# The opening of a Fourier-mixing and ELU kernel: seven steps' events put into one list

## The chip, the cores and the metric

The kernel runs on one core of a Trainium2 chip. The time is the device time of one execution in microseconds (us); the median of several runs is compared.

## The reference

`x` has 8 sequences of 3008 rows and 256 channels. The result is a two-layer perceptron with ELU on the real part of a two-dimensional Fourier transform:

```python
X = np.fft.fft(np.fft.fft(x, axis=1), axis=2).real
h = X.reshape(24064, 256) @ w_in             # w_in 256 x 2048
g = np.where(h > 0.0, h, np.exp(np.minimum(h, 0.0)) - 1.0)
out = g @ w_out                              # w_out 2048 x 256
```

`x` is fp32. The two weights are float64, and the kernel reads them as pairs of 32-bit words.

## The kernel before

**The transform.** `fold_x` (L498) adds and subtracts the mirrored rows and channels of one sequence: four loaded blocks L0 to L3 become the tiles e0 to e3 and o0 to o3 (and, with the short column copies c0 to c3, the sums E0, E2, O0, O2 and the four stationary tiles EO0 to EO3). For the first sequence these run on VectorE. Four `Dft` objects multiply them on TensorE with constant matrices: cosine for even rows (R_even here, R below), sine for even rows (I), cosine for odd rows (R_odd, O below), sine for odd rows (I_odd, J below). A fifth, `x_even` (x), transforms one single channel. Each has two halves of matmuls into two PSUM banks ("even" and "odd"), then `copy` (ScalarE), `unfold` (VectorE, "sum" below), and `plus` and `minus` (VectorE, "up" and "down"), which write the rings Rr, Ir and Rb in SBUF. The channel transform is put into w_in: `fold_chunk` (L427, f below) multiplies a chunk of w_in with a constant matrix, `put_chunk` copies the result to Ws and Wc on ScalarE, and `turn_last_row` and `put_last_row` (wm and wex) or `spread_last_row` (two DMAs) bring one more row into `wex`.

**Weights from 64 bits.** Each weight is read in eight chunks of 512 KB, w0 to w7 for w_in and u0 to u7 for w_out. A chunk is turned into fp32 by `fields` (VectorE: exponent, then mantissa), `power` (ScalarE, three activations), `round` (GpSimd add), and `scale` (VectorE sign, GpSimd product, for w_in also two GpSimd pair sums). Chunk w0 does all on VectorE and the exponent's activation on ScalarE.

**The perceptron.** The ring's columns are taken 256 at a time, eight steps of 256 hidden units per tile, 376 steps in all. A step is: `mm_P` (Wc by Rr into a bank H), `even_part` (V below: VectorE adds the single channel, two instructions), `mm_Q` (Ws by Ir into the same bank), `h_minus` (h: the mirrored rows), `below_plus`, `below_minus`, `exp_plus`, `exp_minus` (b+, b-, x+, x-: ScalarE), `g_plus`, `g_minus` (g+, g-: VectorE). Then the product with w_out: in the first 16 steps `mm_plain` in two halves (Xa, Xb), later a form with fewer products and four GpSimd sums. The first 16 slots alternate between tiles 0 and 1.

**PSUM.** Eight banks: three with the tag H, which P, the weight folds, the odd sine transform and others take in turn, one M, and pA to pD for the output sums. The early transforms borrow pA to pD and M.

**The order.** Most operations go through `pin`, which keeps the program order of an engine. The program order is made by `at(t, fn)`: events are sorted by t, in nominal microseconds where slot n begins at 4.8 n, and called one after another. In the profile such a time lies about 26 us later, and drifts. An event may be a group:

```python
at(-24.4, lambda: fold_now("e1 c1 E0 EO0"))
at(-10.88, w1_chunks[1].fields)      # two VectorE instructions
at(-10.5, lambda: dft_now(I_even, 0, "pC"))
```

DMAs from SP are not pinned, except those of `spread_last_row`. `load_rest` first writes one element of the sine matrix on ScalarE, which depends on x, and then loads that matrix and the next chunks.

Of the kernel before, what the change touches and what calls it, by code (L numbers as in the profile page):

```python
# [25 lines left out]
NE = 377  # L26
# [80 lines left out]
def kernel(  # L107
# [109 lines left out]
    class Chunk:  # L217
# [30 lines left out]
        def fields(self):  # L248

            if not wide:  # L250
                return
            lo, hi, dst = self.parts()
            t = spool.tile([128, 512], I32, tag=self.tmp_tag, bufs=1, name="pow2")
            self.t = t.rearrange("p (a b) -> p a b", a=dst.shape[1])
            pin(
                nc.vector.tensor_scalar(
                    out=self.t, in0=hi, scalar1=0x7FF00000, scalar2=None,
                    op0=ALU.bitwise_and,
                )
            )  # L260
            pin(
                nc.vector.tensor_scalar(
                    out=dst.bitcast(I32), in0=hi, scalar1=0xFFFFF, scalar2=0x100000,
                    op0=ALU.bitwise_and, op1=ALU.bitwise_or,
                )
            )

        def power(self):

            if not wide:  # L270
                return
            act(self.t, self.t, func=AF.Relu, scale=8.0, bias=ebias)
            if self.shared:
                lo, _, dst = self.parts()
                act(lo.bitcast(FP), lo.bitcast(U32), scale=2.0**-52)
                act(dst, dst.bitcast(I32), scale=2.0**-20)

        def round(self):

            if not wide:  # L280
                return
            lo, hi, dst = self.parts()
            if self.shared:
                gtt(dst, lo.bitcast(FP), dst, ALU.add)
                return
            pin(
                nc.vector.scalar_tensor_tensor(
                    out=dst, in0=lo.bitcast(U32), scalar=2.0**-32,
                    in1=dst.bitcast(I32), op0=ALU.mult, op1=ALU.add,
                )  # L290
            )

        def pair(self):

            dst = self.dst()
            gtt(self.ab[:, 0:256], dst[:, 0], dst[:, 1], ALU.add)
            gtt(self.ab[:, 256:512], dst[:, 0], dst[:, 1], ALU.subtract)

        def scale(self):

            self.multiply()
            if self.pairs:
                self.pair()

        def multiply(self):
            if not wide:
                return
            lo, hi, dst = self.parts()
# [5 lines left out]
            )  # L314
            if self.shared:
# [6 lines left out]
                )  # L322
            )
# [124 lines left out]

    def put_chunk(c):
        cols = slice(c * 256, (c + 1) * 256)  # L450
        for n, dst in enumerate((Ws, Wc)):
            act(dst[:, cols], folds[c][:, 256 * n : 256 * n + 256])
# [45 lines left out]
    def fold_x(L, engine_of, pieces):  # L498
# [3 lines left out]
        def op(key, o, a, b, f):  # L502
# [3 lines left out]
            n = o.shape[1]  # L506
            cuts = [n * i // pieces for i in range(pieces + 1)]
            for i in range(pieces):
# [100 lines left out]
    class Dft:  # L609
# [30 lines left out]
        def minus(self):  # L640
# [8 lines left out]
            if self.ri == 0 and not self.kodd and not self.first:  # L649
                vtt(R4[:, self.b : self.b + 1], u[:, 0:1], v[:, 0:1], ALU.subtract)  # L650
# [165 lines left out]

    def h_minus(i):
        S = steps[i]
        S.G = spool.tile([128, GW], FP, tag="G", bufs=3, name="G")
# [22 lines left out]
    def below_plus(i):  # L842
        S = steps[i]
        below(S.G[:, 512:1024], S.H)
# [262 lines left out]
    for load in loads[:5]:  # L1107
# [8 lines left out]
        L_first, lambda key: nc.vector, 1  # L1116
    )

    def fold_now(keys):
        for key in keys.split():  # L1120
            ops[key, 0]()
# [13 lines left out]
    def load_rest():  # L1135
# [7 lines left out]
        for chunk in (w1_chunks[3], w2_chunks[1], w1_chunks[4], w2_chunks[2]):  # L1143
            chunk.load()

    at(-26.9, lambda: fold_now("e3 c3 o3"))
    at(-26.8, w1_chunks[0].fields)
    at(-26.7, w1_chunks[0].power)
    at(-26.6, w1_chunks[0].round)
    at(-26.5, w1_chunks[0].scale)  # L1150
    at(-26.4, lambda: fold_now("e0 c0 e2 c2 E2"))
# [3 lines left out]
    at(-25.5, load_rest)  # L1155
    at(-24.5, begin_x_even)
    at(-24.4, lambda: fold_now("e1 c1 E0 EO0"))
    at(-20.7, lambda: load_mats(1, 1))
    at(-20.6, w1_chunks[5].load)
    at(-20.5, w2_chunks[5].load)  # L1160
    at(-13.2, lambda: fold_chunk(0))
    at(-13.1, lambda: put_chunk(0))
    at(-13.1, lambda: dft_now(state["x_even"], 0, "pC"))
    at(-13.09, lambda: state["x_even"].copy())
    at(-13.08, lambda: dft_now(state["x_even"], 1, "pD"))
    at(-13.0, lambda: dft_now(R_even, 0, "pA"))
    at(-12.9, lambda: dft_now(R_even, 1, "pB"))
    at(-11.1, lambda: fold_now("o0 o2 O2 o1 O0 EO2"))
    at(-11.0, lambda: state["x_even"].unfold())
    at(-10.95, R_even.copy)  # L1170
    at(-10.94, R_even.unfold)
    at(-10.9, R_even.plus)
    at(-10.89, lambda: state["x_even"].plus())
    at(-10.885, lambda: act(Ir[96:128, 0:NE], Rb[96:128, 0:NE]))
    at(-10.88, w1_chunks[1].fields)
    at(-10.87, w1_chunks[1].power)
    at(-10.86, w1_chunks[1].round)
    at(-10.85, R_even.minus)
    at(-10.5, lambda: dft_now(I_even, 0, "pC"))
    at(0.05, lambda: dft_now(I_even, 1, "M"))  # L1180
    at(0.6, lambda: state["x_even"].minus())
    at(0.61, lambda: act(Ir[96:128, NE:RUN], Rb[96:128, NE:RUN]))
    at(-10.84, w1_chunks[1].scale)
    at(1.3, lambda: fold_now("EO1"))

    T = PERIOD
    for chunk, k in (
        (w2_chunks[0], 0),
        (w1_chunks[2], 1),
        (w2_chunks[1], 2),  # L1190
        (w1_chunks[3], 3),
        (w2_chunks[2], 4),
        (w1_chunks[4], 5),
        (w2_chunks[3], 6),
# [9 lines left out]
        first = (  # L1204
            (0.96, 0.96, 0.97, 1.9),
            (2.1, 2.9, 2.91, 4.22),
            (2.95, 2.96, 2.97, 4.2),
            (0.95, 0.96, 0.97, 4.2),
        )
        dt = first[k] if k < 4 else (-0.5, 0.05, 0.06, 2.95)  # L1210
        for d, fn in zip(dt, (chunk.fields, chunk.power, chunk.round, chunk.scale)):
            at(t + d, fn)
    for chunk, t in (
        (w2_chunks[3], 0.5),
        (w2_chunks[4], 0.95),
# [6 lines left out]
    for c in range(1, 8):  # L1222
        at((2 * c - 2) * T + 4.7 if c > 1 else 2.7, lambda c=c: fold_chunk(c))
        t = (2 * c - 1) * T + 0.03 if c > 1 else 3.0
        at(t, lambda c=c: put_chunk(c))
        if c > 1:
            at(t + 0.01, lambda c=c: spread_last_row(c))
    at(-10.6, lambda: turn_last_row(0))
    at(-10.59, lambda: put_last_row(0))
    at(3.15, lambda: turn_last_row(1))  # L1230
    at(T + 0.25, lambda: put_last_row(1))
    for i in range(8):
        at((12.9 + 0.5 * i) * T + 3.6, lambda i=i: sum_weights(i))
    at(2 * T + 4.2, lambda: fold_now("EO3"))
# [9 lines left out]
    for slot in range(total):  # L1244
        i = slot % 2 * 8 + slot // 2 if slot < 16 else slot
        t = slot * T
        begin = (
            (0.0, mm_P),
            (0.4 if slot == 0 else 0.9, even_part),
            (2.17, mm_Q),  # L1250
            (3.55, h_minus),
            (4.2, below_plus),
            (4.8, below_minus),
            (T + 0.01 if slot < 16 else T + 1.5, exp_plus),
            (T + 0.02 if slot < 16 else T + 2.21, exp_minus),
        )
        if slot == 1:
            begin = (
                (0.1 - T, mm_P),
                (0.7 - T, even_part),  # L1260
                (2.6 - T, mm_Q),
                (1.5, h_minus),
                (2.95, below_plus),
                (3.0, below_minus),
                (3.01, exp_plus),
                (3.02, exp_minus),
            )

        X3 = ((3 * T + 0.1 if i % 8 == 0 else 2 * T + 3.05, mm_X3),)
        for dt, fn in begin + (  # L1270
            (T + 2.2, g_plus),
            (T + 2.9, g_minus),
        ) + (
            (
                (2 * T + 0.87, lambda i: mm_plain(i, 0)),
                (2 * T + 3.04, lambda i: mm_plain(i, 1)),
            )
            if i < 16
            else WINOGRAD + X3
        ):  # L1280
            at(t + dt, lambda fn=fn, i=i: fn(i))
# [59 lines left out]
    def begin_folds(b):  # L1341
        state["EO"], state["ops"] = fold_x(state["L"], lambda key: nc.gpsimd, 2)

    steps_b = HALF * 8 // TW
    for t, fn in (
        (-1.8, I_even.copy),
        (0.5, I_even.unfold),
        (0.55, I_even.plus),
        (0.65, I_even.minus),
        (3.1, lambda: dft_now(R_odd, 0, "pA")),  # L1350
        (3.2, lambda: dft_now(R_odd, 1, "pB")),
        (T + 0.005, R_odd.copy),
        (T + 1.9, R_odd.unfold),
        (T + 4.2, R_odd.plus),
        (T + 4.21, R_odd.minus),
    ):
        at(t, fn)
    at_half(3, lambda: I_odd, 0, 0)
    at_half(5, lambda: I_odd, 1, HALF)
# [25 lines left out]
    for b in range(1, NB):  # L1385
# [3 lines left out]
        at(l0 * T + 0.1, lambda b=b: state.update(zip(("L", "loads"), load_x(b))))  # L1389
        for n in range(6):  # L1390
            t = l0 + gap * n if n < 4 else l0
            at(t * T + 0.2, lambda n=n: state["loads"][n]())
# [73 lines left out]
```

## Time and profile before

| what | value |
|---|---|
| median of 7 runs | 1951.14 us (1949.22 to 1953.35) |
| profiled execution, time | 1949.54 us |
| its span | 1947.8 us |
| granted TensorE clock | 0.999 |
| first useful matmul | 14.07 us |
| P of slot 0 | 25.80 us |
| Q of slot 0 | 30.65 us |
| first X (slot 0) | 39.74 us |
| DMA in 14 to 23 us | 406 GB/s |

The profile is one execution. PE is TensorE's matmuls, PEld its weight loads, DVE VectorE, ACT ScalarE, POOL GpSimd, SP the queue that issues most DMAs. A row of the timeline has the start, the busy time, engine, line, operation, output and inputs, and in brackets the idle time before it and what ended it. The line is that of a helper where one records an operation: L410 is every matmul, L416 VectorE's additions of the transforms, L419 GpSimd's, L422 ScalarE's, L504 the folds of x, L256 and L262 a chunk's exponent and mantissa, L310 its sign, L811 V, L821 h, L837 g.

### The profile page before, as it was taken

The page shows a single profiled execution, that of the slowest core. Times are in us where ns is not written, and L with a number is a line of the kernel's source. Part 1 is how long each engine was busy: PE and PEld are TensorE (multiplying, and loading weights), DVE is VectorE, ACT ScalarE, POOL GpSimd, SP SyncE. Part 2 cuts the span into 40 slices and gives each one's busy share as a digit, 9 for nine tenths or more (in the row PEclk, how much of TensorE's full clock was granted, in tenths as well). Part 3 has the DMA queues.
Part 4 walks back from the last instruction along what each step waited for, and adds up shares of the span by engine and source line. Part 5 has one row for each costly group of instructions (what it writes and reads, how often), then busy time and mean ns, then how long its engine had stood idle before and what let it go on. Part 6 is the DMA issues. An engine that isn't in the chain of part 4 may idle for free.

```text
span 1947.8 us, 26994 instructions
## 1 busy us (share of the span) xinstructions
PE 1934.9 (99%) x8912; PEld 1653.1 (85%) x8912; DVE 1298.9 (67%) x2396; ACT 864.8 (44%) x1671; POOL 1376.4 (71%) x1816
## 2 busy tenths in 40 slices
PE   8999999999999999999999999999999999999999
PEld 5788788888888888888888888888888888888887
DVE  8966666766666666666666665676666766667666
ACT  4654444444444444444344444444434444344443
POOL 3888767776678766777677876778667776456655
PEclk9999999999999999999999999999999999999999
DMA  8146110101101121010210202012020010100101
GB/s 313 63 32 49 36 47 20 47 14 30 38 20 44 16 44 28 18 48 12 53 24 13 50 10 59 12 20 58 7 53 11 20 23 14 17 11 11 23 10 24
DMA packets 263290, 70.25 MB, mean 36 GB/s; under 512 B 248606, under 2 KB 249522, under 8 KB 263152
## 3 DMA queue, kind: packets, MB, share of 16 engines
q1 hardware_dynamic: 257360, 55.69, 15.0%
q0 software_dynamic: 3616, 12.59, 2.1%
q8 instruction: 70, 1.15, 0.3%
q14 instruction: 68, 0.56, 0.1%
q10 hardware_dynamic: 2176, 0.26, 0.1%
HBM read 43.66 MB, written 24.80 MB: 35 GB/s over the span
## 4 chain that ended last, share of the span: by engine, by line
PE 94%; DVE 3%; POOL 2%; ACT 1%; DMA 1%; issue 1%; SPq 0%; DVEq 0%
PE H L410 38%; PE pB L410 16%; PE pC L410 16%; PE pD L410 16%; PE pA L410 8%; POOL WT L419 1%; POOL G L419 0%; DMA xl<-in_x_dram 0%; DVE E L811 0%; POOL w L419 0%; DVE o L504 0%; DVE G L837 0%; DVE e L504 0%; DMA xl<-in_x_dram,ix 0%; DVE v L416 0%
## 5 line engine op out<-in xcount | busy, mean ns | idle before, releaser
L419 POOL TENSOR_TENSOR G<-G 128x256 f32<-128x256 f32 x1440 | 1034.9, 728 | 510.6 <-DVE G L837 341.3
L811 DVE SCALAR_TENSOR_TENSOR E<-Rb,wex,H 128x256 f32<-128x256 f32 x752 | 327.7, 477 | 541.5 <-PE H L410 537.3
L422 ACT ACTIVATE G<-H 128x512 f32<-128x512 f32 x376 | 224.5, 597 | 958.7 <-DVE G L821 958.7
L410 PE MATMUL H<-Ir,Ws 128*128 128x256 f32 x1504 | 387.0, 380 | 5.3 <-DVE E L811 4.2
L410 PE MATMUL H<-Rr,Wc 128*128 128x256 f32 x1504 | 386.8, 380 | 0.0
L410 PE MATMUL pC<-G,WT 128*128 128x256 f32 x1440 | 369.6, 379 | 0.0
L410 PEld LDWEIGHTS H<-Rr,Wc 128*128 128x128 f32 x1504 | 284.8, 190 | 55.3 <-issue 3.0
L410 PEld LDWEIGHTS H<-Ir,Ws 128*128 128x128 f32 x1504 | 278.4, 189 | 53.7 <-DVE E L811 6.0
L410 PEld LDWEIGHTS pC<-G,WT 128*128 128x128 f32 x1440 | 273.6, 190 | 37.2
L821 DVE SCALAR_TENSOR_TENSOR G<-E,H 128x512 f32<-128x512 f32 x376 | 256.6, 683 | 41.4 <-POOL G L419 5.0
L837 DVE SCALAR_TENSOR_TENSOR G<-G,H 128x512 f32<-128x512 f32 x376 | 255.7, 680 | 42.5 <-ACT G L422 42.5
L837 DVE SCALAR_TENSOR_TENSOR G<-M,G 128x512 f32<-128x512 f32 x376 | 256.5, 682 | 0.0
L422 ACT ACTIVATE G<-G 128x512 f32<-128x512 f32 x376 | 233.2, 620 | 0.0
L410 PE MATMUL pD<-G,w 128*128 128x256 f32 x784 | 229.4, 379 | 0.6 <-POOL G L419 0.6
L410 PE MATMUL pA<-G,w 128*128 128x256 f32 x784 | 229.3, 379 | 0.0
L410 PE MATMUL pB<-G,w 128*128 128x256 f32 x784 | 229.3, 379 | 0.0
L422 ACT ACTIVATE M<-G 128x512 f32<-128x512 f32 x376 | 224.2, 596 | 0.0
L422 ACT ACTIVATE M<-M 128x512 f32<-128x512 f32 x376 | 221.0, 588 | 0.0
L410 PE MATMUL pB<-G,WT 128*128 128x256 f32 x720 | 214.8, 380 | 0.3
L410 PE MATMUL pD<-G,WT 128*128 128x256 f32 x720 | 214.2, 379 | 0.0
L410 PEld LDWEIGHTS pD<-G,w 128*128 128x128 f32 x784 | 148.9, 190 | 21.2 <-POOL G L419 1.0
L410 PEld LDWEIGHTS pA<-G,w 128*128 128x128 f32 x784 | 148.9, 190 | 20.5 <-issue 0.3
(148 smaller groups left out, 1414.5 us busy)
## 6 DMA issues: line engine op xcount, KB each, us to landing
out_dram<-ot SPq DMA_DIRECT2D x496, 32.0 KB
xl<-in_x_dram SPq DMA_DIRECT2D x16, 512.0 KB
xl<-in_x_dram SPq DMA_DIRECT2D x16, 256.0 KB
out_dram<-ot SPq DMA_DIRECT2D x256, 2.0 KB
Rb<-r SPq DMA_DIRECT2D x10, 376.0 KB
raw<-in_moe_w_in_dram SPq DMA_DIRECT2D x7, 512.0 KB
MC<-dft_mats SPq DMA_DIRECT2D x3, 943.5 KB
raw<-in_moe_w_out_dram SPq DMA_DIRECT2D x4, 512.0 KB
```

Of the source, the lines that this page charges most:

```text
L410: nc.tensor.matmul(out_, lhsT=lhsT, rhs=rhs, start=start, stop=stop, skip_group_check=True)
L419: pin(nc.gpsimd.tensor_tensor(out=o, in0=a, in1=b, op=op))
L422: pin(nc.scalar.activation(out=o, in_=i, func=func, **kw))
L811: nc.vector.scalar_tensor_tensor(out=S.E[:, c], in0=Rb[:, cols(i)], scalar=wex[:, f : f + 1], in1=S.H[:, c], op0=ALU.mult, op1=ALU.add,)
L821: nc.vector.scalar_tensor_tensor(out=two(S.G[:, 0:512])[:, :, ::-1], in0=two(S.E), scalar=2.0, in1=two(S.H), op0=ALU.mult, op1=ALU.subtract,)
L837: nc.vector.scalar_tensor_tensor(out=o, in0=e, scalar=-1.0, in1=h, op0=ALU.add, op1=ALU.max)
```

## The change

The events of the opening, up to slot 6, are replaced by one list, `FRONT`, of some 300 names with 40 nominal times; each name is one operation. Groups are split for this: a chunk's `fields` into `top` and `mantissa` (a, b), its `power` into `power`, `low`, `high` (p, l, d), `round` (R), and `scale` into `sign`, `multiply`, `pair` (s, M, P); `put_chunk` into two halves; the extra column of R's `minus` becomes `half` (R4). The folds e0 and e2 are each cut into rows 0 to 3 (a) and rows 4 and 5 (b). Letters follow the kernel's parts above, with the slot, chunk or block as number: `P0`, `V0`, `Q0`; `I-odd` for the odd half of the even-row sine transform; `L0` to `L3` for the loads of the second sequence from GpSimd.

```diff
-        def fields(self):
+        def top(self):
...
+        def mantissa(self):
...
+            _, hi, dst = self.parts()
...
-            cuts = [n * i // pieces for i in range(pieces + 1)]
+            cuts = cuts_of(key, o.shape[1])
...
+        lambda key, n: (0, 4, n) if key in ("e0", "e2") else (0, n),
...
+    def open_G(S):
+        if not hasattr(S, "G"):
+            S.G = spool.tile([128, GW], FP, tag="G", bufs=3, name="G")
...
     def load_rest():
...
+        load_mats(1, 1)
+        w1_chunks[5].load()
+        w2_chunks[5].load()
...
-    at(-13.1, lambda: dft_now(state["x_even"], 0, "pC"))
-    at(-13.08, lambda: dft_now(state["x_even"], 1, "pD"))
-    at(-13.0, lambda: dft_now(R_even, 0, "pA"))
-    at(-12.9, lambda: dft_now(R_even, 1, "pB"))
-    at(-11.1, lambda: fold_now("o0 o2 O2 o1 O0 EO2"))
...
+    FRONT = (
+        (-20.84, "e3 o3"),
+        (-19.11, "w0a w0b w0p w0R c3"),
+        (-17.62, "w0s w0M"),
+        (-16.21, "e0a e2b o2"),
+        (-14.32, "e2a o0 c2"),
+        (-12.89, "E2 f0 O2"),
+        (-11.63, "xl1 xs e1 x-even"),
+        (-9.8, "e0b c1 o1 c0 x-odd x-copy Wc0"),
+        (-8.58, "E0 Ws0 EO0"),
+        (-7.29, "wm0 wex0 O0 R-odd"),
+        (-5.76, "w1b EO2"),
+        (-4.55, "w2b R-even u0b w2d u0a EO1 w1d"),
+        (-3.25, "I-odd R-copy w1l w1a x-sum u0l"),
+        (-1.92, "w1R R-sum w1p I-even x-down R-up"),
+        (-0.64, "Irc2 w1s u0p P0 x-up I-copy w1M"),
+        (0.82, "R-down O-even Irc I-sum u1l V0"),
+        (2.21, "w1P w2l P1 I-up u0d"),
+        (3.48, "I-down Q0 u0R R4 V1"),
+        (4.76, "f1 h0 b+0 O-copy u0s Q1"),
+        (5.99, "x+0 w2a b-0 u0M O-odd"),
+        (7.24, "Wc1 g+0 x-0 O-sum Ws1"),
+        (8.46, "w2R w2p h1 wm1 g-0 b+1 P2"),
+        (9.82, "wex1 O-down b-1 w2s Xa0 x-1 V2 w2M x+1"),
+        (11.32, "O-up w3l Q2 g-1 w2P g+1 Xb0"),
+        (12.61, "h2 u1a b-2 EO3 u1p f2"),
+        (14.06, "u1b x-2 w3a P3 u1d w3b u1s b+2 Xa1 L"),
+        (15.24, "L0 V3 x+2 Ws2 g-2 w3d u1R Q3 g+2"),
+        (16.44, "w3p u3b Wc2 Xb1 b+3 w3R h3"),
+        (17.88, "w4b b-3 J-even u1M w4l w3s x-3"),
+        (19.2, "P4 x+3 u2l u2b w3M Xa2 u3d V4"),
...
+        (30.87, "V6 w4M Xa4 g+5"),
+        (32.25, "u3s L3 Q6 w4P g-5 Xb4 b+6 h6 J-up u3M"),
+        (33.32, "b-6 J-down"),
+    )
+    front = set()
+    for t, line in FRONT:
+        for n, name in enumerate(line.split()):
+            front.add(name)
+            at(t + 0.001 * n, names[name])
...
-        (w2_chunks[4], 0.95),
+        (w2_chunks[4], 1.65),
```

`xl1` is `load_rest`, `xs` the four small additions that begin `x_even`, `Irc` and `Irc2` ScalarE's copies of rows from Rb to Ir. The events outside the list keep their times; those of the named operations are removed. TensorE's order of the transforms was f0, x, R (even, odd), wm0, I-even, P0, I-odd, P1, Q0, Q1, f1, O-even, wm1, O-odd, P2, Xa0; it becomes f0, x, wm0, R-odd, R-even, I-odd, I-even, P0, O-even, P1, Q0, f1, Q1, O-odd, P2, wm1, Xa0.

## The prediction

> **What bounds the kernel now.** I read the page's busy shares first, then the busy time in stretches, then TensorE's and VectorE's timelines of the opening.
>
> ```profile
> PE 1934.9 (99%) x8912; PEld 1653.1 (85%) x8912; DVE 1298.9 (67%) x2396; ACT 864.8 (44%) x1671; POOL 1376.4 (71%) x1816
> ```
>
> TensorE is busy 99% of the span, so only its idle time can be won. The stretches show where that is; columns are TensorE, weight load, VectorE, ScalarE, GpSimd, granted clock, DMA share, GB/s.
>
> ```profile
> 14.07:23.00 8.93, 8.85 (x45) 5.89 (x44) 8.69 (x15) 1.52 (x5) 0.00 (x0) 1.00 1.04 406
> 23.00:30.00 7.00, 5.15 (x20) 3.59 (x20) 6.19 (x17) 2.60 (x6) 1.47 (x2) 1.00 1.04 396
> 30.00:49.00 19.00, 16.14 (x76) 11.43 (x76) 17.54 (x31) 13.45 (x28) 11.92 (x11) 1.00 0.67 243
> 49.00:72.00 23.00, 23.00 (x107) 18.43 (x105) 21.17 (x36) 14.07 (x27) 17.57 (x17) 1.00 0.38 127
> 72.00:110.00 38.00, 37.52 (x185) 29.28 (x186) 33.76 (x47) 26.02 (x51) 33.39 (x33) 1.00 0.07 15
> ```
>
> Up to 49 us TensorE has holes while VectorE is nearly full; after 49 us TensorE is full. In TensorE's timeline:
>
> ```profile
> 22.42 0.50 PE L410 MATMUL H<-pick,Ws 128*128 128x1 f32 x4
> 24.44 1.52 PE L410 MATMUL pC<-MC,o 128*128 128x189 f32 x6 [1.52 <-issue]
> 25.80 1.02 PE L410 MATMUL H<-Rr,Wc 128*128 128x256 f32 x4
> ...
> 30.65 1.10 PE L410 MATMUL H<-Ir,Ws 128*128 128x256 f32 x4 [1.06 <-DVE Ir L416]
> 33.01 1.10 PE L410 MATMUL H<-Ir,Ws 128*128 128x256 f32 x4 [1.26 <-DVE E L811]
> ...
> 39.74 1.97 PE L410 MATMUL pA<-G,w 128*128 128x256 f32 x8
> 42.66 1.13 PE L410 MATMUL H<-Ir,Ws 128*128 128x256 f32 x4 [0.95 <-DVE E L811]
> ```
>
> A matmul of 256 columns takes 0.216 us from start to start (eight in the chain's 1.73 us), so ends in this view are late by the pipeline. Counted by columns, the holes from the first useful matmul (14.07) to Q of slot 3 (49.23) are 1.70 before 24.44, 1.22 before 30.65, 1.42 before 33.01, 1.12 before 42.66, and a dozen of about 0.1 (a matmul released by a semaphore, or following 64-column ones): **6.65 us idle, 28.5 us of work**. All four large ones wait for VectorE. What later holes there are (0.64 us at 106.86; 1.39 at 232.34; 0.76 at 1445.93) lie after the list.
>
> **The change, part by part.** *Same work.* TensorE's matmuls up to Q and X of slot 4-6 are the same set in both orders; so are ScalarE's, GpSimd's, and the bytes loaded. Added are two VectorE instructions: e0 and e2 are cut at four of six rows, so that each part needs one load. No row shows them; by elements the 0.88 us step of a whole fold of 768 divides into 0.58 and 0.30, and at worst each extra instruction adds the 0.1 us step of the smallest ones (xa to xg). I take nothing lost, since VectorE waits for a load right behind them anyway.
>
> *VectorE, step by step.* Steps from start to start in the trace: fold 0.88 (0.98 where it needs the one before), exponent or mantissa 0.34, sign 0.60, the two E parts (V) 0.79, h or g 0.60, an unfold 0.52, a ring row 0.46. Landings are the sixteenth semaphore increments: first part of L0 9.59, the rest 11.58; L2's two parts 10.39 and 11.39; L1 13.28 and 14.51. The first seven operations keep their times (5.18 to 10.1). Then:
> - e0a at 10.1; e2b waits to 11.48 (before, VectorE stood from 10.16 to 11.67). o2, e2a, o0, E2, O2: to 16.1, xs to 16.5.
> - e1, e0b, c1, o1, E0, EO0: to 20.75. O0, w1b, EO2: to 22.95. w2b, u0b, u0a, EO1, w1a: to 25.25. x-sum, R-sum, x-down, R-up: to 27.25.
> - w1s, x-up, R-down, I-sum, V0: to 30.1; I-up to 30.65; I-down, R4, V1: to 31.95.
> - h0 (after Q0), u0s, w2a, g+0, O-sum, h1, g-0: to 35.85; O-down, w2s, V2: to 37.75; O-up, g-1, g+1: to 39.45.
> - h2, u1a, EO3, u1b, w3a, w3b, u1s: to 43.0; V3 to 43.8, or 44.5 with one port conflict (below).
>
> *TensorE from that*, a transform's halves costing 1.27 and 1.90, P, Q 0.86, X 1.73, a weight fold 0.9:
> - f0 14.07 (the warm-up matmuls end there, as before). x-even waits for xs: 16.6, **0.75 idle**. x-odd, wm0: to 20.2. R-odd waits for EO0: 20.85, **0.65**. R-even, I-odd (its matrix landed at 22.61, EO2 at 22.95), I-even: to 27.25.
> - P0 waits for R-up: 27.4, **0.15**. O-even, P1: to 30.4. Q0 waits for I-up: 30.75, **0.35**. f1 (GpSimd's pairs end at 30.6), Q1, O-odd, P2, wm1: to 36.75.
> - Xa0 (g-0 at 35.85), Q2 (V2 at 37.75), Xb0, f2 (GpSimd's w2P at 39.7; bank free at 39.45), P3, Xa1: to 44.9. Q3 about 45.0.
>
> Idle is 1.9 plus about 0.6 of the small ones, 2.5 against 6.65. **Q3 moves from 49.23 to 45.0: 4.2 us.** P0 itself is later (25.80 before): between P0 and Q0 now stands a transform with its data ready, and Q1 no longer waits alone for V1. What is late next is VectorE's V3, with 0.4 us to spare.
>
> *The banks and queues.* H has three banks, so each new one waits for the third before: P2 for g+0 (34.1 against 35.55), f2 for g+1 (39.45 against 41.2), J-even for g+2 (45.7 against 47.5). None binds. ScalarE, in order, has b+0, O-copy, x+0, b-0, Wc1, x-0, Ws1, w2p, b+1, wex1 from 31.8 to 36.95 at about 0.55 each; wex1 holds V2 until 36.95, counted above. On SP, u4's load waits for f1 and has b=1's x loads behind it; f1 moves from 34.04 to 31.75, so both go earlier. L1 to L3 stand later in GpSimd's list, 1 to 1.3 us each, but their folds begin in slot 6. The last row's spread after Ws2 (43.8) is two DMAs, 4 us by the rows of before, 2 us ahead of V4.
>
> *After Q3* the work to the end of slot 4's X is 22.7 us of matmuls; before it took 49.23 to 71.91, with 0.6 of holes, so TensorE already sets the pace, and V4, V5, V6 come out 0.5 to 4 us early in the same walk. The gain is kept at 4.2.
>
> **A rule against the change.** GpSimd's conversions now start at 25.4 instead of 28.45 and lie beside VectorE's. The rows of before:
>
> ```profile
> 40.43 1.39 DVE L310 SCALAR_TENSOR_TENSOR pow<-raw,pow 128x512 int32<-128x512 int32 x1
> ...
> 45.72 0.70 DVE L310 SCALAR_TENSOR_TENSOR pow<-w,pow 128x512 int32<-128x512 int32 x1
> 46.32 2.07 DVE L504 TENSOR_TENSOR o<-o,o 128x768 f32<-128x768 f32 x1
> ```
>
> A sign step takes 0.68 alone and 1.39 beside GpSimd, a fold 2.07 instead of 0.96; from 37 to 48 us such stretches sum to 2.5 us. h, g and V, which read PSUM, are never longer. The Trainium skill ("SBUF — State Buffer", "Who interferes with whom") says that a VectorE instruction with two SBUF inputs, or in a two-port mode, and a GpSimd instruction reading SBUF exclude each other for a whole instruction. By the rule, the nine such VectorE steps between Q0 and V3 could each wait half of GpSimd's 1.30, 5.9 us: Q3 at about 49.8 and no gain. By the rows it is 2.5: Q3 at 46.4, gain 2.8. By place it is less: in my walk GpSimd is idle from 39.7 to 42.4, under u1a, EO3, u1b and w3a; only u1s overlaps, 0.7. I take 0.7, and keep 0 and 5.9 as ends.
>
> **Rivals.**
> - *VectorE stays the bound* through those stretches: 2.5 us or more of them before V3. For: VectorE has 17.54 of 19 us busy in 30-49. Against: the idle gap just named. 1951.14 - 2.8 = 1948.3.
> - *The gain is given back* in 72-110, should GpSimd or VectorE limit that stage. For: 33.39 and 33.76 of 38 us busy. Against: TensorE idles only about 1 us there. 1950.
> - *Slower: the sine matrix comes late.* I-odd now needs it at 24.05; it landed at 22.61, behind two weight chunks that had overtaken it, in a stretch where DMA moves about 400 GB/s without a gap. Each further chunk let past costs 1.35 us (24.91, 26.26, 27.62), one for one on I-odd, I-up and Q0. From a landing of 28.3 the change loses; with all six chunks of the loading step ahead (20.35 + 8.1 + 2.3 = 30.8, and a later cosine matrix behind it) Q0 is 6.8 late: net +2.6, 1953.7. Against: the order in the loading step is unchanged, and ScalarE's write that releases the matrix waits for the same landing at 14.51.
> - *The list not kept?* Each engine's operations follow program order, so the order holds; its times are only sort keys.
>
> **How the numbers follow.** The profiled execution took 1949.54 (1947.8 span and 1.7 around it); 1949.54 - 4.2 = 1945.3. The median shown is 1.6 higher, so 1951.14 - 4.2 = **1946.9**. About 0.2% (3.9 us, below 1947.2 or above 1955.0) is what a measurement here can tell. Chances: forecast 0.50, VectorE still bound 0.24, given back 0.08, matrix late 0.18. The forecast alone spans 1944.3 (no conflict, and the 0.64 and small holes to 107 gone: 6.8) to 1947.6; with the rivals, 1944.3 to 1952.5. Faster 0.50 (the forecast), within 0.38 (VectorE, given back, and the third of the late matrix where few chunks pass), slower 0.12 (its rest, where the cosine matrix or a wait behind it adds to the 2.6).
>
> **What would show it.** TensorE's timeline: P0 near 27.4, Q0 near 30.7, Q3 near 45.0, no hole over 0.8 after 14.07; V3 ending by 44.9; xs at 16.1; EO3 at 0.96, not 2. I am wrong if I-odd waits for a DMA, if a weight fold waits for GpSimd, or if holes of the first 49 us return after 72.

## The result and the profile after

The changed kernel takes 1945.21 us (median of 15 runs) against 1950.35 (35 runs of before): ratio **0.9973, interval 0.9967 to 0.998**, or 5.1 us less. The profiled executions differ by 4.3 us (1945.24 against 1949.54; spans 1943.5 and 1947.8); the one of before lies 0.8 below its median.

The first four stretches of the prediction's table, now of the changed kernel, in the same columns (TensorE, weight load, VectorE, ScalarE, GpSimd, granted clock, DMA share, GB/s):

```profile
14.07:23.00 8.93, 7.85 (x40) 5.34 (x36) 8.86 (x18) 1.83 (x7) 0.00 (x0) 1.00 1.04 407
23.00:30.00 7.00, 7.00 (x30) 5.02 (x29) 7.00 (x18) 6.56 (x13) 4.04 (x5) 1.00 1.04 392
30.00:49.00 19.00, 19.00 (x93) 14.72 (x93) 16.63 (x35) 14.33 (x30) 13.29 (x11) 1.00 0.78 277
49.00:72.00 23.00, 22.21 (x106) 17.36 (x105) 18.56 (x32) 14.18 (x28) 16.36 (x15) 1.00 0.32 91
```

TensorE is full from 23 to 49 us, where it had 4.7 us of visible gaps. ScalarE does 6.56 us of work in 23-30 instead of 2.60, GpSimd 4.04 instead of 1.47: conversions of weights moved forward into time that those engines spent waiting. Two places are worse: 14-23 (7.85 instead of 8.85, of which 0.6 is work of f0 that now lies before 14.07) and 49-72 (22.21 instead of 23.00). In TensorE's timeline after:

```profile
16.25 1.54 PE L430 MATMUL pC<-MC,xe 128*128 128x189 f32 x6 [0.86 <-DVE xe L436]
...
26.73 1.02 PE L430 MATMUL H<-Rr,Wc 128*128 128x256 f32 x4
27.59 1.43 PE L430 MATMUL pA<-MC,e 128*128 128x188 f32 x6
28.86 1.03 PE L430 MATMUL H<-Rr,Wc 128*128 128x256 f32 x4
29.77 1.13 PE L430 MATMUL H<-Ir,Ws 128*128 128x256 f32 x4
...
44.16 1.03 PE L430 MATMUL H<-Ir,Ws 128*128 128x256 f32 x4
...
68.86 1.10 PE L430 MATMUL H<-Rr,Wc 128*128 128x256 f32 x4 [0.79 <-DVE Ir L436]
```

P0, O-even, P1 and Q0 follow each other with no hole. Q of slot 3, at 49.23 before, starts at 44.16. Then P of slot 7 waits for VectorE. The table shows the course: the first five lines give when a step starts, and a negative difference means earlier.

| start of | before | after | difference |
|---|---|---|---|
| P, slot 0 | 25.80 | 26.73 | +0.93 |
| Q, slot 0 | 30.65 | 29.77 | -0.88 |
| Q, slot 3 | 49.23 | 44.16 | -5.07 |
| Q, slot 6 | 69.32 | 64.30 | -5.02 |
| P, slot 7 | 73.01 | 68.86 | -4.15 |
| end of the span less P of slot 7 | 1874.77 | 1874.61 | -0.16 |

From P of slot 7 to the end, all ten kernels below take 1874.5 to 1875.1 us in their profiles. Whatever the list does, it does before 73 us.

### The profile page after: what moved, and what is told of

Read it like the earlier page. It is cut to its first block, busy times and chain, and to the rows that moved or that the text cites. A ratio compares the mean times of both kernels' runs of the same rounds, so it can differ in the third digit from the quotient of the medians.

```text
span 1943.5 us, 26993 instructions
## 1 busy us (share of the span) xinstructions
PE 1933.1 (99%) x8912; PEld 1653.5 (85%) x8912; DVE 1293.0 (67%) x2398; ACT 865.6 (45%) x1671; POOL 1377.0 (71%) x1816
## 4 chain that ended last, share of the span: by engine, by line
PE 94%; DVE 2%; POOL 2%; ACT 1%; DMA 1%; issue 1%; DVEq 0%; POOLq 0%
PE H L430 38%; PE pB L430 16%; PE pC L430 16%; PE pD L430 16%; PE pA L430 8%; DMA xl<-in_x_dram,ix 1%; POOL WT L439 1%; POOL G L439 1%; DVE G L869 0%; DVE E L839 0%; DVE e L527 0%; POOL w L439 0%; DVE v L436 0%; ACT G L442 0%; DVE pow L310 0%
```

## The experiments

Each was timed against the kernel before on the same chip. Three chips were used, and before's median on them was 1949.97 to 1950.09 us (1950.35 in the result above), so a few tenths of a microsecond between an experiment and the changed kernel say little. "Q3" is the start of Q of slot 3 in the profile of that run.

### TensorE's order undone

`pe_old` has this order on TensorE (first part shown; - is the list's, which has wm1 ahead of P2, not behind it as said under "The change") and the list's order on the others:

```diff
-f0 x-even x-odd wm0 R-odd R-even I-odd I-even P0 O-even P1 Q0 f1 Q1 O-odd wm1 P2 Xa0
+f0 x-even x-odd R-even R-odd wm0 I-even P0 I-odd P1 Q0 Q1 f1 O-even wm1 O-odd P2 Xa0
```

> The list with TensorE's operations in the order of before (R before wm0, I-even before P0, I-odd after it, Q0, Q1, f1, O-even, wm1, O-odd, and J-odd before P6); the other engines keep the new order. Theory (VectorE's order makes the gain): Q of slot 3 stays within 1 us of 44.2, time within 1 us of the changed kernel, about 5 below before; the 0.96 us hole ahead of P7 shrinks to 0.2 since J-odd is earlier. Rival (TensorE's order and the bank rotation make it): Q of slot 3 goes back to 47 to 49 and the time to within 2 us of before.

Measured: 1953.27 us, ratio 1.0013 (1.0004 to 1.0022), **slower than before**; Q3 at 52.94. Neither theory said so. In its profile, TensorE:

```profile
35.71 1.54 PE L430 MATMUL pA<-MC,e 128*128 128x188 f32 x6
39.82 0.61 PE L430 MATMUL H<-pick,Ws 128*128 128x1 f32 x4 [2.57 <-ACT Ws L442]
40.29 3.40 PE L430 MATMUL pB<-MC,e 128*128 128x376 f32 x6
```

and ScalarE:

```profile
34.23 0.60 ACT L442 ACTIVATE G<-H 128x512 f32<-128x512 f32 x1 [1.67 <-DVE G L853]
37.34 0.33 ACT L442 ACTIVATE anti<-pA 128x188 f32<-128x188 f32 x1 [2.52 <-PE pA L430]
```

ScalarE stands at 34.83 for O-copy (`anti<-pA`), since O-even now comes after f1. Behind it in its queue are x+0, b-0, Wc1, x-0 and Ws1. TensorE's next matmul, wm1, needs Ws1, and so TensorE waits for a queue that waited for TensorE: 2.7 us. Then the six matmuls of O-odd take 3.40 us, where the same form takes about 2.1 in the other runs: the granted clock had fallen (shown below). About 1.5 us of Q3's delay are not the order's: in this execution w0's load let VectorE begin its conversion at 9.41 instead of 7.07, and xs came at 17.16 instead of 15.68.

The clock does not fall in every execution. Of the eleven, three have a mean clock of 1.000 and took 1950.5 to 1951.2 us; the others have 0.999 or 0.998 and took 1952.1 to 1955.2. Where no fall shows, this kernel is thus within 1.3 us of before (1949.99), as the rival said; "slower" holds for the mixture.

`pe_old_fit` keeps TensorE's old order and takes that wait away:

```diff
 ScalarE
-b+0 O-copy x+0 b-0 Wc1 x-0 Ws1
+b+0 x+0 b-0 Wc1 x-0 Ws1 O-copy
 VectorE
-g+0 O-sum h1 g-0
+g+0 h1 g-0 O-sum
```

> TensorE's order of before again, but ScalarE's O-copy moved behind Ws1 and VectorE's O-sum behind g-0, so that no queue stands for O-even, which this order brings after f1. If the order of one engine is bad only where another's does not fit it, the 2.7 us hole before wm1 and the fall of the clock go: Q of slot 3 at 45 to 46 instead of 52.9, time 1 to 2.5 above the changed kernel, 3 to 4 below before. If TensorE's order itself carries the gain: Q of slot 3 at 48 or later, time within 1 of before.

Measured: 1948.30 us, ratio 0.9994 (0.9985 to 1.0003), an interval that does not tell it from before; Q3 at 46.84, clock 1.00. It lies between the two theories. The hole before wm1 is gone, as expected of the fit; but Q3 is 2.7 later than with TensorE's new order, more than the 1 to 2 I gave it, and the time is 3.1 above the changed kernel instead of 1 to 2.5. Its holes of 0.71, 1.24, 0.65 and 0.33 us lie before 32.2: R-even stands for EO0 with wm0 behind it, I-even for x-sum (its bank), and P0 for R-up right after I-even, with no ready transform in between. This 2.7, the wait of 2.7, the clock (3.41 us at half speed, 1.7) and the late load (1.5) make 8.6 of the 8.8 us by which Q3 of `pe_old` is late.

### The other engines' order undone

`pe_new_rest_old`: TensorE in the list's order, VectorE, ScalarE and GpSimd in that of before, EO1 moved up because O-even needs it.

```diff
-e3 o3 w0a w0b w0R w0s w0M e0a e2b o2 e2a o0 E2 O2 xs e1 e0b c1 o1 E0 EO0 O0 w1b EO2 w2b u0b u0a EO1
+e3 o3 w0a w0b w0R w0s w0M e0a e0b e2a e2b E2 xs e1 c1 E0 EO0 o0 o2 O2 o1 O0 EO2 EO1 x-sum R-sum
```

> The converse: TensorE in the list's order, VectorE, ScalarE and GpSimd in the order of before, with EO1 alone moved up behind EO2 because O-even now stands ahead of P1. Theory: VectorE idles for ScalarE and meets GpSimd as before, Q of slot 3 at 47.5 to 49.5, time within 2 us of before. Rival: Q of slot 3 near 44 to 45, time about 5 below before.

Measured: 1949.96 us, ratio 0.9997 (0.9988 to 1.0006); Q3 at 49.55. The theory's numbers held (Q3 to 0.1), the rival's did not. TensorE's order alone brings nothing. With `pe_old_fit`, the answer to "which engine's order makes the gain" is: neither alone. Of the 5.07 us at Q3, about 2.4 stay when TensorE's order is undone and the queues are fitted to it, none when the other engines' is undone.

### One more VectorE instruction

`eo1_twice`:

```diff
-        (-4.55, "w2b R-even u0b w2d u0a EO1 w1d"),
+        (-4.55, "w2b R-even u0b w2d u0a EO1 EO1 w1d"),
```

> The changed kernel with the fold EO1 done twice (the same result, one VectorE instruction of 0.88 us more, ahead of the transforms' unfolds). Theory (VectorE's chain sets the pace up to V3): P0, Q0 and V3 0.9 later, Q of slot 3 0.6 to 0.9 later, time 0.5 to 0.9 above the changed kernel. Rival (TensorE or loads set it): less than 0.2 on Q of slot 3.

Measured: 1947.49 us, ratio 0.9984 (0.9975 to 0.9993), 2.3 above the changed kernel's median; Q0 and Q3 both 1.5 later (31.27, 45.66). That is more than the 0.6 to 0.9 expected, and in this execution VectorE had even reached xs 0.59 earlier. The rest is in VectorE's and GpSimd's rows:

```profile
24.47 1.52 DVE L256 TENSOR_SCALAR pow<-raw 128x512 int32<-128x512 int32 x1
```

```profile
24.15 1.55 POOL L439 TENSOR_TENSOR w<-raw,w 128x512 f32<-128x512 f32 x1 [17.34 <-ACT raw L442]
```

In the changed kernel the same two, w1a and w1R, stand like this:

```profile
24.07 0.42 DVE L256 TENSOR_SCALAR pow<-raw 128x512 int32<-128x512 int32 x1
```

```profile
24.74 1.31 POOL L439 TENSOR_TENSOR w<-raw,w 128x512 f32<-128x512 f32 x1 [17.62 <-ACT raw L442]
```

w1a, pushed back by the second EO1, now starts after GpSimd's w1R has, and waits for it: 1.52 us instead of 0.42. 0.87 + 1.10 - 0.59 is 1.4, which is Q3's delay to 0.1. VectorE's chain thus sets the pace one for one, and part of its price is whether a step begins before or after GpSimd's.

### The fold moved beside GpSimd

`eo3_early`:

```diff
-        (9.82, "wex1 O-down b-1 w2s Xa0 x-1 V2 w2M x+1"),
+        (9.82, "wex1 O-down b-1 w2s Xa0 x-1 V2 EO3 w2M x+1"),
...
-        (12.61, "h2 u1a b-2 EO3 u1p f2"),
+        (12.61, "h2 u1a b-2 u1p f2"),
```

> The changed kernel with the fold EO3 moved from between u1a and u1b, where GpSimd was idle, to behind V2, where GpSimd does w2M and w2P. Conflict theory: EO3 takes 1.8 to 2.3 instead of 0.95, O-up and g-1, g+1 come 2 us later and the fold f2 waits for its bank; Q of slot 3 0.6 to 1.2 later, time as much above the changed kernel. Rival (no conflict, only order): EO3 takes 0.95, Q of slot 3 within 0.2 of 44.16.

Measured: EO3 as `eo3_early` has it, and as the changed kernel has it:

```profile
36.78 1.54 DVE L527 TENSOR_TENSOR o<-o,o 128x768 f32<-128x768 f32 x1
```

```profile
39.77 0.95 DVE L527 TENSOR_TENSOR o<-o,o 128x768 f32<-128x768 f32 x1
```

It waits for the end of w2M (37.51) and then runs, so 1.54 and not the 1.8 to 2.3 expected; a hole of 0.61 appears before Xb0, which needs O-up behind it. Q3 is at 44.47, 0.3 later, or 0.7 with xs having come 0.40 earlier in this execution. The time is 1945.47 (0.9976, 0.9966 to 0.9986), not distinguishable from the changed kernel: the hole before P of slot 7 took up the rest (0.53 instead of 0.96). The conflict is shown, its price here is small.

### The folds uncut, and the clock

`no_cut`:

```diff
-        lambda key, n: (0, 4, n) if key in ("e0", "e2") else (0, n),
+        lambda key, n: (0, n),
```

> The changed kernel with e0 and e2 whole again (one instruction each, in the places of e0a and e2a). Theory: e0 waits for all of L0 (landed 11.58 before), so VectorE idles about 1.5 us there instead of 0.8, and everything up to Q of slot 3 is 0.5 to 0.8 later, less 0.3 of slack before V3: Q of slot 3 at 44.4 to 44.9, time 0.3 to 0.8 above the changed kernel. Rival (the cut is what brings the gain): 2 us or more.

Measured: 1946.21 us, 0.9981 (0.9972 to 0.999), 1.0 above the changed kernel: more than the 0.3 to 0.8 expected and half of what the rival asks. In the profile xs is 1.1 later but Q3 2.26 later (46.42). A hole of 2.19 us before x-even is followed by matmuls at half rate (same columns, clock the third from the right):

```profile
15.00:17.00 2.00, 0.37 (x4) 0.00 (x0) 2.00 (x5) 0.01 (x1) 0.00 (x0) 1.00 1.05 378
17.00:19.00 2.00, 1.64 (x5) 1.64 (x6) 1.93 (x6) 0.00 (x0) 0.00 (x0) 0.62 1.07 396
19.00:21.00 2.00, 2.00 (x4) 1.05 (x4) 1.97 (x3) 0.78 (x3) 0.00 (x0) 0.53 1.04 430
```

`no_cut_fill` puts six matmuls on zeros into that hole:

```diff
+    names["fill"] = lambda: [
+        mm(idle, zero, zero[:, 0:1].to_broadcast([128, 512]), True) for _ in range(6)
+    ]
...
-        (-12.89, "E2 f0 O2"),
+        (-12.89, "E2 f0 fill O2"),
```

> The kernel with whole e0 and e2, and six warm-up matmuls on zeros (1.3 us, results unused) between f0 and x-even, in the 2.2 us hole after which the granted clock fell to 0.53. If the fall of the clock was part of the 2.3 us that the whole folds cost: clock 1.00 throughout 17 to 23, Q of slot 0 about 1.1 after that of the changed kernel instead of 2.4 (30.7 to 31.1), time 0.7 to 1.3 below the run without the fill. If the folds alone cost it: Q of slot 0 stays at 32.1.

```profile
17.00:19.00 2.00, 1.72 (x8) 1.34 (x9) 1.97 (x5) 0.14 (x1) 0.00 (x0) 1.00 1.08 398
```

In the profile the clock stays at 1.00, Q0 comes 0.8 after the changed kernel's instead of 2.4, and the span falls from 1946.2 to 1944.5. But the median does not fall: 1946.48 (0.9982, 0.9973 to 0.9991) against 1946.21. The mean clock, measured in every run, says why. Eight of the eleven runs of `no_cut` show 1.000 and took 1945.8 to 1946.5; three, the profiled one among them, show 0.999 and took 1947.6 to 1948.0. A stretch of 3.41 us at half speed loses 1.7 us of full clock, or 0.0009 of the span, so none of the eight can have had one, and 1.7 us is also what the two groups differ by. (0.999 alone would not prove a fall: the profile of before shows it from a low stretch after its last matmul.) So the uncut folds by themselves cost about 0.9 us, and a fall of the clock, in some executions, 1.7 more. What the zeros do is not shown: without them eight of eleven kept the clock, with them nine show 1.000 and two 0.999 (1947.15 and 1948.09).

### Two edits that were open after the profile

`e2a_first` takes the part of e2 whose load lands first ahead of the other:

```diff
-        (-16.21, "e0a e2b o2"),
-        (-14.32, "e2a o0 c2"),
+        (-16.21, "e0a e2a e2b o2"),
+        (-14.32, "o0 c2"),
```

> The changed kernel with e2a, whose load lands first, ahead of e2b. VectorE's 0.78 us wait before e2b should fall to 0.2 or less, and everything that VectorE sets come earlier by 0.4 to 0.6: Q of slot 0 at 29.2 to 29.4, Q of slot 3 at 43.6 to 43.8, time 0.4 to 0.6 below the changed kernel. Rival (loads or TensorE set the opening): no change.

`j_early` moves J's ring rows into VectorE's wait for ScalarE:

```diff
-        (32.25, "u3s L3 Q6 w4P g-5 Xb4 b+6 h6 J-up u3M"),
-        (33.32, "b-6 J-down"),
+        (32.25, "u3s L3 Q6 w4P g-5 J-up J-down Xb4 b+6 h6 u3M"),
+        (33.32, "b-6"),
```

> The changed kernel with J-up and J-down ahead of h6, where VectorE stood 2.4 us for ScalarE, instead of behind it. Theory: P of slot 7 waited 0.96 us only for J-down to free its bank; the hole falls to 0.2, P of slot 7 at 68.1, time 0.7 to 0.8 below the changed kernel. Rival (another reader of the bank, or GpSimd's pairs of w4, hold it): the hole stays.

> Both of these edits. If they add up: P of slot 7 at 67.5 to 67.8, time 1.1 to 1.4 below the changed kernel, some 6.2 below before. If one eats the other: no better than the better of the two.

In VectorE's timeline of the changed kernel e2b waits 0.78 us for its load; in `e2a_first` e0a, e2a and e2b, merged into one row, follow each other:

```profile
11.26 0.43 DVE L527 TENSOR_TENSOR e<-xl 128x256 f32<-128x256 f32 x1 [0.78 <-DMA xl<-in_x_dram,ix]
```

```profile
9.57 1.62 DVE L527 TENSOR_TENSOR e<-xl 128x512 f32<-128x512 f32 x3
```

Further on, in the changed kernel, h6 waits 2.44 us, and J-down, which frees P7's bank, comes last:

```profile
65.99 0.69 DVE L853 SCALAR_TENSOR_TENSOR G<-E,H 128x512 f32<-128x512 f32 x1 [2.44 <-ACT G L442]
66.60 0.54 DVE L436 TENSOR_TENSOR Ir<-bs,H 127x376 f32<-127x376 f32 x1
67.05 0.87 DVE L256 TENSOR_SCALAR pow<-raw 128x512 int32<-128x512 int32 x1
67.85 0.41 DVE L268 TENSOR_SCALAR w<-raw 128x512 int32<-128x512 int32 x1
68.18 0.53 DVE L436 TENSOR_TENSOR Ir<-H,bs 127x376 f32<-127x376 f32 x1
```

In `j_early` J's two rows start at 63.47 and 63.92, h6 still at 66.00, and P of slot 7 follows the fold before it at once:

```profile
63.47 0.54 DVE L436 TENSOR_TENSOR Ir<-bs,H 127x376 f32<-127x376 f32 x1
63.92 0.54 DVE L436 TENSOR_TENSOR Ir<-H,bs 127x376 f32<-127x376 f32 x1
66.00 0.69 DVE L853 SCALAR_TENSOR_TENSOR G<-E,H 128x512 f32<-128x512 f32 x1 [1.53 <-ACT G L442]
```

```profile
68.00 1.13 PE L430 MATMUL H<-Rr,Wc 128*128 128x256 f32 x4
```

| run | time | ratio to before (interval) | Q3 | P of slot 7 |
|---|---|---|---|---|
| the change | 1945.21 | 0.9973 (0.9967 to 0.998) | 44.16 | 68.86 |
| `e2a_first` | 1944.91 | 0.9972 (0.9961 to 0.9982) | 43.07 | 67.78 |
| `j_early` | 1944.65 | 0.9971 (0.996 to 0.9982) | 44.16 | 68.00 |
| `both` | 1944.21 | 0.9969 (0.9957 to 0.9981) | 43.32 | 67.16 |

In the profiles both do what was expected or more: in the first VectorE's wait of 0.78 is gone (the other 0.3 of Q3 is an earlier first load), in the second the hole of 0.96, and P of slot 7 comes 1.7 earlier with both. The medians move by 0.3, 0.6 and 1.0, in the order expected and each a little less than expected, within intervals that overlap; the profiles, not the medians, show the two causes. `both` is the fastest kernel measured.

## Why the prediction was right

*What bounds it.* Right. All of the difference lies before P of slot 7, in holes of TensorE.

*The sum.* 4.2 us forecast; 5.1 by the medians, 4.3 by the profiles. The holes from f0 to Q3 came out at 2.4 us (2.5 forecast, from 6.65), with one at 1.06 (0.75 forecast) and one at 0.39 (0.65). Q3 is at 44.16, not 45.0, since VectorE began e0a at 9.80 and not 10.1 and reached xs at 15.68 and not 16.1, and since V3 met no conflict. (That f0 began at 13.44, the warm-up matmuls having ended earlier, only made the hole before x-even longer.) P0 came at 26.73 (27.4 forecast), Q0 at 29.77 (30.75). The wait before e2b was 0.78, as worked out. Of the signs named, "no hole over 0.8" failed twice: 1.06 before x-even and 0.96 before P of slot 7.

*After Q3* the step failed. "The gain is kept at 4.2" took V4, V5 and V6 as the only things that could be late and the banks as not binding, since I followed the rotation to J-even only. P of slot 7 takes a bank that J-down must free, and 0.9 us went back there. That the total was near all the same is luck: Q3 was early by nearly as much as was lost behind it.

*Port conflicts.* One conflict of 0.7 at u1s was priced; there was none (0.69): u1s began at 41.65, GpSimd's u1R at 41.91, and it was GpSimd that took 1.58 instead of 1.30:

```profile
41.65 0.69 DVE L310 SCALAR_TENSOR_TENSOR pow<-w,pow 128x512 int32<-128x512 int32 x1
```

```profile
41.91 1.58 POOL L439 TENSOR_TENSOR w<-w 128x512 f32<-128x512 f32 x1 [1.19 <-ACT w L442]
```

The rule of the Trainium skill ("SBUF — State Buffer", "Who interferes with whom"), that the second to start waits for the whole of the first, agrees with w1a in `eo1_twice` and EO3 in `eo3_early`, which end 0.3 and 0.8 after the GpSimd instruction they met. A forecast by it needs to know which of the two starts first; the walk by place gave that better than the mean of the rows (2.5) or half of each GpSimd instruction (5.9). VectorE's part of the gain is also there: the sign steps and EO3 that took 1.39 and 2.07 before take 0.68 and 0.95.

*The rivals.* VectorE still bound: no, it had V3 at 42.63, waiting for P3. Given back in 72-110: no, the end less P of slot 7 is the same. The sine matrix late: no; its load was issued at 14.38 (14.76 before).

*The reason* was too narrow. I wrote of the new order as VectorE's steps and treated TensorE's as following; undoing either alone costs half of the gain or all of it.

## What to carry to other kernels

When several engines run in a fixed order, walk all the queues together, up to the last operation that the change moves and one turn of the buffers beyond it: the one place I did not walk is where 0.9 us went back. Moving operations on one engine alone can be worse than moving none, when another engine's queue then stands for a result that comes later, with the next operation's operand behind it. In a stretch where VectorE sets the pace, spend its waits: put the operation whose load lands first ahead, and those whose inputs are ready into the waits of others.

## What was not expected of the hardware

A hole of TensorE can cost more than its length. After 2.19 us (`no_cut`) and 2.74 us (`pe_old`) the clock record shows 3.41 us at 0.5, from 17.46 and from 41.03; after holes of 1.79 us (`eo1_twice`) and 1.70 (before) it shows none. `pe_old`, then `eo1_twice`:

```profile
41.00:43.00 2.00, 2.00 (x5) 1.11 (x4) 0.00 (x0) 1.97 (x4) 0.00 (x0) 0.51 0.91 358
```

```profile
23.00:30.00 7.00, 5.36 (x23) 3.62 (x22) 6.97 (x15) 4.74 (x10) 2.83 (x2) 1.00 1.04 395
```

In the first TensorE is busy throughout with five matmul records in 2 us; 41-43 in the changed kernel has thirteen. By the mean clocks of the eleven runs of `no_cut`, such a fall comes in some executions only. The Trainium skill ("TensorE: Matmul & The Clock Gate", Part 1) has the clock halved after an idle window of about 3.4 us, on a window that runs free of the kernel. The length of the slow stretch agrees, but here neither hole filled a window: of the 3.41 us before 17.46 f0 took the first 1.1 and the hole 2.19, and in the 3.41 us before 41.03 lie 2.2 of the 2.74. So for these two executions a window that is idle for 2.2 us was enough. That the window lies elsewhere in each execution would fit the fall coming only in some; no run here shows it.
